# Another order of the SBUF pools in a fused convolution and squared-ReLU MLP kernel

## The chip, the core and the metric

The kernel runs on one NeuronCore of a Trainium2 chip. The core has TensorE (PE, the matmul array, with its weight loads shown as PEld), VectorE (DVE), ScalarE (ACT), GpSimd (POOL) and SyncE (SP), which here only issues DMAs. All of them work on SBUF, an on-chip memory of 128 partitions; a tile has up to 128 rows, one per partition, and in each partition it takes a run of bytes that begins at the same address. PSUM is the small memory into which TensorE writes. The metric is the device time of one execution in microseconds (us), median of three runs.

## What is computed

The input x is 8 sequences of 4096 tokens with 192 features, in float32. First a causal convolution over 7 tokens with softmax weights, one set for each of 8 heads of 24 features; then a two-layer MLP over the 32768 tokens:

```python
w = softmax(weight)                     # (8 heads, 7 taps)
a[t, d] = sum_k w[head(d), k] * x[t - 6 + k, d]
h = a @ w_in                            # 192 -> 2048
g = s * relu(h)**2 + b
out = g @ w_out                         # 2048 -> 192
```

## The kernel before

Features lie on partitions. The 192 features are 128 (tiles with A in their name) and 64 (tiles with B, two blocks of 512 tokens stacked on 128 partitions). The tokens are worked in superblocks of 1024, and each superblock n in two blocks j of 512 tokens. For each block, the 2048 hidden units are worked in 8 pairs p of 128-unit chunks.

The matmuls run in float32r. To reach float32's accuracy, each operand is split into a high and a low part, and the product is made of three: high with low, high with high, low with high. Line numbers are those of the profile:

- `Tokens.load` reads xA and xB from HBM, `conv` (L149, L151) makes the convolution on VectorE into accA and accB, `split_A` and `split_B` write the high and low parts into sA and tB, and `swap` copies them by DMA with the upper and lower 64 partitions exchanged into wA and wB.
- `first` (L526) makes the hidden layer h of one (n, j, p) in PSUM: 18 matmuls of 64 rows x 512 columns, in 9 pairs. One of a pair works on partitions 0 to 63, the other on 64 to 127, at the same time. What streams is sA, wA, tB or wB; what is loaded as weight is a 128-column chunk of the tile W.
- ScalarE takes relu(h) out of PSUM into a tile q (L540) and squares it in place (L547). VectorE rounds it to qh (L549) and takes the rest into ql (L554).
- `second` (L609) multiplies qh and ql with the output weights in W and WB: 20 matmuls of 64 x 512, in 10 pairs, summed in PSUM over the 8 pairs p. It lags behind `first` by LAG = 2 entries of a queue. For superblock 0 `second_whole` (L571 to L578) does the same with 128-row matmuls, and the last entry of all is done by `last` (L668 to L687).
- At the end of a block ScalarE and GpSimd scale and sum the halves (L629 to L642), and SP stores them.
- The weights arrive as float64; the class `Widen` turns them into high and low float32r parts in W and WB during superblock 0. `head` prepares the first tokens, with a part of the convolution on TensorE in plain float32 (L245).

So 2048 bytes in each partition are streamed by every matmul (512 columns of 4 bytes), and 512 bytes (128 columns) are loaded as its weight.

Where the tiles lie is decided by the order of the pools. A pool holds, for each name of a tile, as many buffers as its `bufs` says; pools take their room one after the other, in the order in which they are made, and inside a pool the names follow in the order of their first use, each buffer rounded up to 32 bytes. The pools before, in order: const (W, WB and seven small tiles), raw, wordp, xin, xs, act, qs, outs. In the program built from it, addresses within a partition are:

| tiles | first address | beyond a multiple of 2048 |
|---|---|---|
| W (40960 bytes), WB (8192) | 16512, 57472 | 128 |
| tap, minus, tmax, tsum, sb, bb, bias | 65664 to 66399 | |
| t (2 x 3072), c (3072), words (3 x 6144) | 66400 | 864 or 1888 |
| xA (2 x 4120), xB (2 x 2072) | 94048 | 1888 to 1984 |
| accA, sA, wA, tB, wB, hiB, accB (xs) | 106464 | 2016 |
| q (act), qh and ql (qs), oA, oC, oB, oB2, oA2 (outs) | 155616 | 2016 |

The tiles of xs, act, qs and outs have 2048 or 4096 bytes, so that one offset holds for all their buffers.

Of the kernel before, what the change touches and what calls it, by code (L numbers as in the profile page):

```python
# [9 lines left out]
F32 = mybir.dt.float32  # L10
F32R = mybir.dt.float32r
# [6 lines left out]
P = 128  # L18
# [3 lines left out]
LAG = 2  # L22
# [3 lines left out]
TWICE = (4, 6)  # L26

WARM = (BLK, BLK // 2, BLK // 2)


TOP_MIN = struct.unpack("<f", struct.pack("<I", (1023 - 127) << 20))[0]
# [4 lines left out]
def conv_attention_then_squared_relu_mlp(  # L36
# [25 lines left out]
    NPAIR = weights64.shape[0]  # L62
    K = taps.shape[2]
    PAD = K - 1
    DB = D - P
    NF = 2 * NPAIR
    SUP = 2 * BLK
    NSUP = T // SUP

    const = ctx.enter_context(tc.tile_pool(name="const", bufs=1))  # L70
    raw = ctx.enter_context(tc.tile_pool(name="raw", bufs=2))
    wordp = ctx.enter_context(tc.tile_pool(name="wordp", bufs=3))
    xin = ctx.enter_context(tc.tile_pool(name="xin", bufs=2))
    xs = ctx.enter_context(tc.tile_pool(name="xs", bufs=2))
    act = ctx.enter_context(tc.tile_pool(name="act", bufs=3))
    qs = ctx.enter_context(tc.tile_pool(name="qs", bufs=LAG + 3))
    outs = ctx.enter_context(tc.tile_pool(name="outs", bufs=3))
    ps_h = ctx.enter_context(tc.tile_pool(name="ps_h", bufs=2, space=bass.MemoryType.PSUM))
    ps_o = ctx.enter_context(tc.tile_pool(name="ps_o", bufs=2, space=bass.MemoryType.PSUM))

# [176 lines left out]
    CI = 3 * P  # L257
    CB = CI + 2 * P
    CT = CB + 2 * DB
    W = const.tile([P, NPAIR, 2, CB], F32R, name="W")  # L260
    WB = const.tile([P, NPAIR, 2, 2 * DB], F32R, name="WB")

    def w_in(part, p, chunk, rows):
        return W[rows, p, part, chunk * P : (chunk + 1) * P]

    def w_outA(part, f, rows=slice(0, P)):
        return W[rows, f // 2, part, CI + f % 2 * P :][:, 0:P]

    def w_outB(f, rows=slice(0, P)):
        return WB[rows, f // 2, f % 2, :]  # L270

    class Widen:
# [7 lines left out]
        def parts(self, v):  # L280

            z = min(self.hi, CB)
            yield (*(W[:, self.p, k, self.lo : z] for k in range(2)), v[:, 0 : z - self.lo])
            if self.hi > CB:
                v = v[:, CB - self.lo :].rearrange("p (j d) -> p j d", j=2)
                yield (*(WB[:, self.p, :, k * DB : (k + 1) * DB] for k in range(2)), v)

# [46 lines left out]
    def fetch(p, a=0, z=None):  # L334
        if a == 0:
            words[p] = wordp.tile([P, CT, 2], I32, name="words")
        z = z or CT
        nc.sync.dma_start(
            words[p][:, a:z].rearrange("p f w -> p (f w)"), w_words[p, :, 2 * a : 2 * z]
        )  # L340

    idle = act.tile([P, 2, BLK], F32, name="q")[:, 0, 0:P]
    nc.gpsimd.memset(idle, 0.0)
    tap = const.tile([P, 2, K], F32, name="tap")
    nc.sync.dma_start(tap, taps)
    tapA, tapB = tap[:, 0, :], tap[:, 1, :]
    tok = {0: Tokens(0)}
# [2 lines left out]

    ident = act.tile([P, 2, BLK], F32, name="q")[:, 0, 0:P]
    make_identity(nc, ident)
    minus = const.tile([P, P], F32R, name="minus")
    tmax = const.tile([P, 2], F32, name="tmax")
    tsum = const.tile([P, 2], F32, name="tsum")

    nc.scalar.activation(tsum, idle[:, 0:2], AF.Exp)
    nc.vector.reduce_max(tmax, tap, axis=AX.X)
# [8 lines left out]

    fetch(0, CI, CT)
    fetch(1)
    sb = const.tile([P, 1], F32, name="sb")  # L370
    bb = const.tile([P, 1], F32, name="bb")
    nc.sync.dma_start(sb, s.unsqueeze(0).to_broadcast([P, 1]))
    nc.sync.dma_start(bb, b.unsqueeze(0).to_broadcast([P, 1]))

    def head():
# [4 lines left out]
        warm = ps_o.tile([P, BLK], F32, name="acc1")  # L380
        for cols in WARM:
            nc.tensor.matmul(
# [90 lines left out]
    def column_sums(k):  # L473
# [8 lines left out]
        for o, w in (  # L482
            (sumA, W[:, k, :, CI:CB]),
            (sumB[:, DB:].rearrange("p (j d) -> p j d", j=2), WB[:, k, :, :]),
        ):
            before = W[:, 0, :, CI:CB] if o is sumA else WB[:, 0, :, :]
            before = before.bitcast(F32) if k == 1 else o
# [6 lines left out]
            nc.vector.tensor_tensor(b[:, 0:DB], b[:, 0:DB], b[:, DB:P], op=ALU.add)  # L494


    bias = const.tile([P, 3], F32, name="bias")

    unbiased = []

# [343 lines left out]
```

## Time and profile before

| | |
|---|---|
| median of 3 runs | 2298.05 us (2297.62 to 2298.07) |
| the profiled execution | 2297.88 us, span 2296.1 us |
| TensorE clock granted | 1.000 |
| HBM read, written | 31.64 MB, 25.17 MB |

The span goes from the first to the last instruction that the profiler recorded on the core. A row of the chain of work gives the start and the length of a piece in us, the engine, what it wrote, the line and the number of instructions; a row of the groups gives busy time in us and the mean of one instruction in ns. Three numbers with strokes between them are the shortest, the median and the longest duration of a group in ns. The rows themselves stand in the prediction.

### The profile page before, as it was taken

How to read it: one execution, taken by the hardware profiler on the slowest of the kernel's cores; microseconds unless marked ns; L12 is line 12 of the kernel's file. 1: busy time of each engine (PE TensorE's matmuls, PEld its weight loads, DVE VectorE, ACT ScalarE, POOL GpSimd, SP SyncE). 2: the span in 40 equal slices, each digit the busy share in tenths (PEclk: the TensorE clock that was granted, in tenths of full speed). 3: DMA queues.
4: the chain of work that ended last, by engine and by line, in shares of the span. 5: the costliest groups of instructions: out<-in, count | busy, mean ns of one | idle time of the engine just before them, and what ended most of it. 6: DMA issues, size and time to landing. Idle time of an engine off the chain costs nothing.

```text
span 2296.1 us, 45081 instructions
## 1 busy us (share of the span) xinstructions
PE 2289.9 (100%) x19330; PEld 1829.1 (80%) x19330; DVE 1755.8 (76%) x1995; ACT 1287.5 (56%) x1410; POOL 317.0 (14%) x205
## 2 busy tenths in 40 slices
PE   9999999999999999999999999999999999999999
PEld 6788888888888888888888888888888888888887
DVE  8898777777777787777877777777777777777764
ACT  8755555555555556455555555555555555555554
POOL 0021101101111011110110111101101111011110
PEclk9999999999999999999999999999999999999999
DMA  5113112121121111111111212112121121111110
GB/s 175 38 40 86 42 38 61 49 54 42 43 56 51 51 42 50 49 52 52 44 49 47 55 49 53 47 40 60 49 54 43 43 56 51 51 43 43 42 38 17
DMA packets 46168, 117.51 MB, mean 51 GB/s; under 512 B 7760, under 2 KB 8016, under 8 KB 45968
## 3 DMA queue, kind: packets, MB, share of 16 engines
q1 hardware_dynamic: 45824, 114.50, 18.9%
q8 instruction: 151, 2.47, 0.5%
q14 instruction: 49, 0.40, 0.1%
q10 hardware_dynamic: 144, 0.13, 0.0%
HBM read 31.64 MB, written 25.17 MB: 25 GB/s over the span
## 4 chain that ended last, share of the span: by engine, by line
PE 99%; DVE 1%; DMA 0%; ACT 0%; SPq 0%; issue 0%; DVEq 0%
PE acc L609 50%; PE h L526 47%; PE acc L571 0%; PE acc L572 0%; PE acc L577 0%; PE acc L576 0%; PE acc L578 0%; DVE accA L151 0%; DMA xA<-in_xA 0%; DVE t L303 0%; DVE t L300 0%; DVE t L296 0%; DVE oB L671 0%; ACT W L310 0%; PE acc L668 0%
## 5 line engine op out<-in xcount | busy, mean ns | idle before, releaser
L540 ACT ACTIVATE q<-h 128x1024 f32<-128x1024 f32 x512 | 526.3, 1028 | 966.0 <-PE h L526 958.8
L549 DVE CAST qh<-q 128x1024 fp32r<-128x1024 f32 x497 | 372.8, 750 | 455.6 <-ACT q L547 454.6
L554 DVE TENSOR_TENSOR ql<-q,qh 128x1024 fp32r<-128x1024 f32 x512 | 656.7, 1283 | 56.9 <-ACT qh L549 3.3
L609 PE MATMUL acc<-qh,W 64*128 64x512 f32 x3960 | 622.0, 392 | 0.0
L547 ACT ACTIVATE q<-q 128x1024 f32<-128x1024 f32 x512 | 543.0, 1061 | 16.0
L609 PEld LDWEIGHTS acc<-qh,W 64*128 64x128 f32 x3960 | 370.9, 184 | 91.1
L526 PE MATMUL h<-sA,W 64*128 64x512 f32 x3072 | 441.8, 392 | 0.0
L526 PE MATMUL h<-wA,W 64*128 64x512 f32 x3072 | 441.2, 392 | 0.0
L526 PE MATMUL h<-tB,W 64*128 64x512 f32 x1536 | 439.6, 392 | 0.0
L526 PE MATMUL h<-wB,W 64*128 64x512 f32 x1536 | 439.6, 392 | 0.0
L609 PE MATMUL acc<-ql,WB 64*128 64x512 f32 x1980 | 391.2, 392 | 0.0
L609 PE MATMUL acc<-qh,WB 64*128 64x512 f32 x1980 | 391.1, 392 | 0.0
L609 PE MATMUL acc<-ql,W 64*128 64x512 f32 x1980 | 391.0, 392 | 0.0
L633 POOL TENSOR_TENSOR oB<-oB,oB 128x512 f32<-128x512 f32 x61 | 115.4, 1892 | 1731.7 <-ACT oB L632 1731.7
L151 DVE SCALAR_TENSOR_TENSOR accA<-xA,tap,accA 128x512 f32<-128x512 f32 x378 | 340.5, 901 | 6.8
L526 PEld LDWEIGHTS h<-sA,W 64*128 64x128 f32 x3072 | 287.3, 184 | 72.7 <-issue 1.5
L526 PEld LDWEIGHTS h<-wA,W 64*128 64x128 f32 x3072 | 287.7, 184 | 70.6
L526 PEld LDWEIGHTS h<-tB,W 64*128 64x128 f32 x1536 | 282.6, 184 | 47.1 <-issue 0.2
L526 PEld LDWEIGHTS h<-wB,W 64*128 64x128 f32 x1536 | 282.6, 184 | 23.7
L609 PEld LDWEIGHTS acc<-ql,WB 64*128 64x128 f32 x1980 | 185.5, 184 | 46.0 <-DVE ql L554 0.6
L609 PEld LDWEIGHTS acc<-ql,W 64*128 64x128 f32 x1980 | 185.5, 184 | 45.5
L609 PEld LDWEIGHTS acc<-qh,WB 64*128 64x128 f32 x1980 | 185.5, 184 | 45.4
(115 smaller groups left out, 1035.6 us busy)
## 6 DMA issues: line engine op xcount, KB each, us to landing
wA<-sA SPq DMA_DIRECT2D x126, 256.0 KB, 3.7
outT<-oA SPq DMA_DIRECT2D x63, 256.0 KB, 2.0
wB<-tB SPq DMA_DIRECT2D x60, 256.0 KB, 3.5
xA<-in_xA SPq DMA_DIRECT2D x24, 515.0 KB, 3.6
xB<-in_xB SPq DMA_DIRECT2D x32, 259.0 KB, 2.7
oC<-oB SPq DMA_DIRECT2D x61, 128.0 KB, 2.2
outT<-oC SPq DMA_DIRECT2D x60, 128.0 KB, 2.3
words<-in_w SPq DMA_DIRECT2D x7, 768.0 KB, 6.0
```

The lines of the kernel that those rows point to most:

```text
L151: nc.vector.scalar_tensor_tensor(acc, src, w[:, k : k + 1], acc, op0=ALU.mult, op1=ALU.add)
L526: nc.tensor.matmul(h[:, i, :], w_in(w, p, chunk[0], rows), chunk[part], start=start, stop=stop)
L540: nc.scalar.activation(q, h, AF.Relu)
L547: nc.scalar.activation(q, q, AF.Square)
L549: cast(qh, q)
L554: nc.vector.tensor_tensor(ql, q, qh.bitcast(F32), op=ALU.subtract)
L609: nc.tensor.matmul(accs[to + 2 * i], w(f, r), q[r, f % 2, :], start=start and f == 0, stop=stop and f == ends[i],)
L633: nc.gpsimd.tensor_tensor(o[1], o[1], o[3], op=ALU.add)
```

## The change

The seven small tiles are made first, directly behind the pool const, and an eighth, `gap`, of 296 floats, which nothing writes or reads. Then come the pools qs, xs, act and outs; W and WB move into a pool of their own, wide_w, behind these; raw, wordp and xin, whose buffers have 3072, 6144, 4120 and 2072 bytes, come last. Tiles, buffer counts, instructions and their order stay as they are.

```diff
+GAP = 296
...
     const = ctx.enter_context(tc.tile_pool(name="const", bufs=1))
+    tap = const.tile([P, 2, K], F32, name="tap")
+    minus = const.tile([P, P], F32R, name="minus")
+    tmax = const.tile([P, 2], F32, name="tmax")
+    tsum = const.tile([P, 2], F32, name="tsum")
+    sb = const.tile([P, 1], F32, name="sb")
+    bb = const.tile([P, 1], F32, name="bb")
+    bias = const.tile([P, 3], F32, name="bias")
+    const.tile([P, GAP], F32, name="gap")
+    qs = ctx.enter_context(tc.tile_pool(name="qs", bufs=LAG + 3))
+    xs = ctx.enter_context(tc.tile_pool(name="xs", bufs=2))
+    act = ctx.enter_context(tc.tile_pool(name="act", bufs=3))
+    outs = ctx.enter_context(tc.tile_pool(name="outs", bufs=3))
+    wide_w = ctx.enter_context(tc.tile_pool(name="wide_w", bufs=1))
     raw = ctx.enter_context(tc.tile_pool(name="raw", bufs=2))
     wordp = ctx.enter_context(tc.tile_pool(name="wordp", bufs=3))
     xin = ctx.enter_context(tc.tile_pool(name="xin", bufs=2))
-    xs = ctx.enter_context(tc.tile_pool(name="xs", bufs=2))
-    act = ctx.enter_context(tc.tile_pool(name="act", bufs=3))
-    qs = ctx.enter_context(tc.tile_pool(name="qs", bufs=LAG + 3))
-    outs = ctx.enter_context(tc.tile_pool(name="outs", bufs=3))
...
-    W = const.tile([P, NPAIR, 2, CB], F32R, name="W")
-    WB = const.tile([P, NPAIR, 2, 2 * DB], F32R, name="WB")
+    W = wide_w.tile([P, NPAIR, 2, CB], F32R, name="W")
+    WB = wide_w.tile([P, NPAIR, 2, 2 * DB], F32R, name="WB")
...
-    tap = const.tile([P, 2, K], F32, name="tap")
...
-    minus = const.tile([P, P], F32R, name="minus")
-    tmax = const.tile([P, 2], F32, name="tmax")
-    tsum = const.tile([P, 2], F32, name="tsum")
...
-    sb = const.tile([P, 1], F32, name="sb")
-    bb = const.tile([P, 1], F32, name="bb")
...
-    bias = const.tile([P, 3], F32, name="bias")
```

## The prediction

> **What bounds the kernel now.** I read the page from its first lines, then the chain that ended last, then the waits, and only then single instructions.
>
> ```profile
> span 2296.1 us, 45081 instructions
> PE 2289.9 (100%) x19330; PEld 1829.1 (80%) x19330; DVE 1755.8 (76%) x1995; ACT 1287.5 (56%) x1410; POOL 317.0 (14%) x205
> ...
> PEclk9999999999999999999999999999999999999999
> ...
> PE 99%; DVE 1%; DMA 0%; ACT 0%; SPq 0%; issue 0%; DVEq 0%
> ```
>
> TensorE (PE) is busy all the time and is 99% of the chain, at the full granted clock. A busy PE alone proves little, since its ends are modelled; so the next question is whether it ever waits for anybody, and at what pitch its matmuls follow each other. The list of waits, longest first, answers the first half:
>
> ```profile
> POOL oB L633 <- ACT oB L632: 1731.7, 60, 79.3
> ACT q L540 <- PE h L526: 958.8, 372, 4.7
> DVE qh L549 <- ACT q L547: 454.6, 332, 3.7
> ...
> PEld h L526 <- issue: 1.7, 4, 0.8
> ```
>
> The long waits are those of other engines, ScalarE's for PE's hidden layer among them; PE's own weight loads waited 1.7 us in total in the first matmul stage. So everybody waits for PE, and the time is the number of matmuls times their pitch. The number comes from the groups by line (each pair of 64-row matmuls runs side by side, one on the upper and one on the lower 64 partitions):
>
> ```profile
> L609 PE MATMUL acc<-qh,W 64*128 64x512 f32 x3960 | 622.0, 392 | 0.0
> L526 PE MATMUL h<-sA,W 64*128 64x512 f32 x3072 | 441.8, 392 | 0.0
> L526 PE MATMUL h<-wA,W 64*128 64x512 f32 x3072 | 441.2, 392 | 0.0
> L526 PE MATMUL h<-tB,W 64*128 64x512 f32 x1536 | 439.6, 392 | 0.0
> L526 PE MATMUL h<-wB,W 64*128 64x512 f32 x1536 | 439.6, 392 | 0.0
> L609 PE MATMUL acc<-ql,WB 64*128 64x512 f32 x1980 | 391.2, 392 | 0.0
> L609 PE MATMUL acc<-qh,WB 64*128 64x512 f32 x1980 | 391.1, 392 | 0.0
> L609 PE MATMUL acc<-ql,W 64*128 64x512 f32 x1980 | 391.0, 392 | 0.0
> ...
> L571 PE MATMUL acc<-qh,WB 128*128 128x512 f32 x32 | 13.2, 412 | 0.0
> ```
>
> L526 has 9216 of them, 4608 pairs; L609 has 9900, 4950 pairs; the first block's second stage has five lines of 32 full-height matmuls (L571 stands for them), 160; `last` adds 10 full-height ones. Together 9728 steps. The pitch comes from the chain, whose rows give a start and a length:
>
> ```profile
> 102.42 2.55 PE acc L609 x20
> 104.98 2.10 PE h L526 x18
> ...
> 171.68 4.67 PE acc L609 x40
> 207.15 4.67 PE acc L609 x40
> ...
> 2228.75 4.67 PE acc L609 x40
> ```
>
> Nine pairs of L526 take 2.10 us, 233.3 ns a pair. One block of 512 tokens is 8 x 9 + 8 x 10 = 152 pairs; from 171.68 to 2228.75 there are 58 blocks, so a pair takes 2057.07 / (58 x 152) = 233.34 ns, for all tiles and throughout the run. 9728 x 233.33 ns = 2269.8 us. The first hidden-layer matmul starts at 17.3 us:
>
> ```profile
> L526 PE MATMUL h<-sA,W x3072: 385/391/502, 17.3 to 2282.5; 64*128 64x512 f32 x192
> ...
> 2290.11 0.75 DVE oB L671
> ```
>
> 2269.8 + 17.3 leaves 9.0 us of the span of 2296.1: about 6.0 behind the last matmul (2290.1 to the end) and 3.0 for changes between 64-row and 128-row matmuls and short stalls. The profiled execution took 2297.88 us, 1.8 more than its span, and the median of the three runs is 2298.05; I forecast against 2298.05 and carry the 1.8 along unchanged.
>
> **The change, part by part.** No instruction, wait, queue or buffer count is added, removed or moved: the diff creates the same tiles in other pools and another order, so only addresses inside a partition differ. Nothing is issued by a moved step, and no queue (SP's or POOL's) is passed. In the kernel before, W starts at byte 16512 and the small tiles and the odd-sized pools follow (t 3072 bytes, xA 4120, xB 2072); therefore all tiles from accA on, which hold everything the matmuls stream, start at 2016 beyond a multiple of 2048, and W's chunks at 128 beyond a multiple of 512. After: 64 (tap) + 512 (minus) + 5 x 32 (the five smallest) + 1184 (gap) = 1920, and 16512 + 1920 = 18432 = 9 x 2048. All of qs, xs, act and outs are made of 2048- and 4096-byte buffers, so they and, behind them, W (139264 = 68 x 2048) and WB start at multiples of 2048. Each streamed operand is 2048 bytes long: before, each crosses one 2048-byte boundary 32 bytes after its start; after, none does. t, c, words, xA and xB come last, at other offsets than before.
>
> *VectorE, ScalarE, POOL and DMA: 0.* The convolution is a natural test of VectorE, for its seven taps read the same tile shifted by 4 bytes each:
>
> ```profile
> L151 DVE SCALAR_TENSOR_TENSOR accA<-xA,tap,accA x378: 737/752/1791, 5.6 to 2209.4; 128x512 f32<-128x512 f32 x189
> L151 DVE SCALAR_TENSOR_TENSOR accB<-xB,tap,accB x186: 743/752/754, 81.9 to 2187.2; 128x512 f32<-128x512 f32 x186
> ```
>
> All 186 of accB's lie between 743 and 754 ns, whatever the shift and buffer: 1.5% at most. Where that reaches the path, in the 17.3 us ahead of the first hidden-layer matmul, 1.5% is 0.26 us at most, up or down; I take 0. Elsewhere these engines are covered by PE, and the cover is wide:
>
> ```profile
> 200.00:236.00 36.00, 36.00 (x312) 28.91 (x310) 28.95 (x34) 19.61 (x21) 4.62 (x3) 1.00 0.25 67
> ```
>
> In that stretch VectorE (the third busy time) does 28.95 us of work in 36, and ScalarE 19.61: VectorE would have to become 24% slower before PE waited. The swaps by DMA (wA<-sA, 3.7 us to land on the page) are issued while the convolution runs ahead, a superblock of two 35.5 us blocks before use.
>
> *The weight load: 0.* W's chunks lie 512 bytes apart, so in the kernel before they already start at four different places within 2048 bytes, and one chunk in four (at 1664) crosses a boundary; every pair has the same pitch all the same. And the load is hidden. The one place where loads bind is L507, whose moving operand is a single column:
>
> ```profile
> 160.45 0.19 PEld L609 LDWEIGHTS acc<-qh,WB 64*128 64x128 f32 x2
> 160.56 0.19 PEld L609 LDWEIGHTS acc<-ql,WB 64*128 64x128 f32 x2
> 160.79 0.19 PEld L609 LDWEIGHTS acc<-qh,WB 64*128 64x128 f32 x2
> ```
>
> With nothing streaming, the next load starts 0.11 us after the one before; behind a streamed matmul it waits 0.23. So a load takes some 0.11 us of the 0.233 and is not what sets the pitch.
>
> *The streamed operand: unknown, and the whole case.* The pitch of 233.3 ns is that of streaming 512 columns of float32r. The head's plain float32 matmuls give something to compare:
>
> ```profile
> 5.77 3.60 PE L245 MATMUL acc<-xB,q 128*128 128x512 f32 x8
> ...
> L245 PE MATMUL acc<-xB,q x14: 590/592/697, 4.4 to 10.1; 128*128 128x512 f32 x14
> ```
>
> Eight in 3.60 us, the last 0.592 long: (3.60 - 0.592) / 7 = 429.7 ns for 512 columns. If float32 goes at exactly half the rate of float32r, a pair could take 214.9 ns, and 233.3 holds 18.4 ns (8%) that the slower stream doesn't show. Whether these 18.4 ns hang on the address, no row of before can say, for every float32r operand there has the same offset. Bounds: the change takes away between 0 and 18.4 ns per step, 0 to 9728 x 18.4 = 179.0 us; and below nothing, as no reason excludes a loss. I take 0, by the nearest rows: the convolution's shifts on VectorE, the four places of the weights, and L245 itself, whose taps stream the token tile from seven offsets, each across a 2048-byte boundary, at one duration (590 to 592 ns but for the first). Nowhere in this trace does an address show in a duration.
>
> [...]
>
> Sum: 0 (other engines) + 0 (weights) + 0 (stream) = **2298.0 us**.
>
> **The rivals.**
>
> *The stream does pay for its address: faster.* For it: the 18.4 ns are there in every step without exception, as a fixed start at 2016 would make them, and float32 at half the rate could hide the same bubble. Against it: a constant of the float32r path would look just the same. All removed: 2298 - 179 = 2119 us. Half removed: 2298 - 89 = 2209. Nothing else becomes late at once: at 214.9 ns the 36 us of the stretch above shrink to 33.2, and VectorE has 28.95 in it; but its slack falls from 7 us to 4, so stalls of VectorE would be next. [...]
>
> *Weights and stream now collide: slower.* A load starts beside the matmul it runs under. Before, the load starts at 128 and the stream at 2016, 352 bytes apart modulo 512; after, both start at a multiple of 512. If the two reads hinder each other when they begin at the same offset, each step grows. Bounds: 0 to the whole load of 0.11 us; the nearest row is the 18.4 ns by which the stream is already late, so I price it at as much again: 2298 + 179 = 2477 us. It decides from 0.47 ns per step on (4.6 us in all). Against it: before, the relation of the two offsets modulo 2048 takes four values, and none shows in the pitch.
>
> *The change doesn't do what it says.* The gap tile is never written. If it got no room, the squares would start at 17248, which is 864 beyond a multiple of 2048: the streams would cross a boundary as before, and the time would be 2298 in any of these worlds.
>
> **How the numbers follow.** Same, by the forecast: 0.45; same because the gap gets no room: 0.03; faster: 0.39; slower: 0.13. About 0.2%, 4.6 us, is what a measurement of this kernel can tell from no change. The likeliest case's own range is 2293.5 to 2302.6. The cases of no change hold only 0.48, so the range for 8 in 10 has to take in the faster case with its full bound: 2119 to 2302.6; the slower case, 0.13, is left out. Chances: faster 0.39, same 0.48, slower 0.13.
>
> **What would show it.** The chain's rows of nine pairs of L526: 2.10 us if I am right, 1.93 if the full 18.4 ns go, over 2.10 if loads and stream collide. The distance of two neighbouring blocks' rows of x40: 35.47 us now, 32.7 in the faster case. VectorE's taps should stay at 743 to 754 ns, and the first hidden-layer matmul should start at 17.3 us within 0.3. If the pitch changes at all, the step "streamed operand: 0" is what failed. If PE starts to wait for VectorE, the pitch fell further than VectorE's slack allowed.

## The result and the profile after

The changed kernel takes 2234.55 us (median of 4 runs, 2234.44 to 2234.66) against 2298.01 for the kernel before (now the median of four runs): a ratio of 0.9724, 95% interval 0.9709 to 0.9740. It is 63.5 us faster. Its page, first lines and chain:

```profile
span 2232.9 us, 45081 instructions
...
PE 2226.4 (100%) x19330; PEld 1829.1 (82%) x19330; DVE 1753.5 (79%) x1995; ACT 1286.4 (58%) x1410; POOL 317.8 (14%) x205
...
PE 98%; DVE 1%; ACT 1%; DMA 0%; issue 0%; SPq 0%; DVEq 0%
```

As many instructions on every engine as before, the busy times of VectorE, ScalarE and GpSimd as before within 0.3%, and PE still busy throughout. So it isn't that somebody waits less: PE itself has become faster. The chain of the changed kernel in order of time (start and length in us) says by how much; L526 and L609 are now L531 and L614:

```profile
104.21 2.04 PE h L531 x18
106.25 2.27 PE acc L614 x20
...
169.09 4.53 PE acc L614 x40
203.55 4.53 PE acc L614 x40
...
2201.84 4.53 PE acc L614 x40
```

Nine pairs take 2.04 us where they took 2.10. From 169.09 to 2201.84 are 59 blocks of 152 pairs, 226.67 ns a pair against 233.33. Over 9728 steps that is 64.8 us, and the span fell by 63.2. The other 1.6 us were given back as new short stalls in superblock 0 and just behind it, the largest of them near 100 us, where superblock 0 goes over into superblock 1. The waits of PE and of its weight loads, changed kernel first, then the kernel before (us in total, times, longest):

```profile
PE acc L614 <- DVE ql L559: 0.4, 1, 0.4
...
PEld acc L614 <- DVE ql L559: 1.3, 2, 0.8
```

```profile
PEld acc L609 <- DVE ql L554: 0.6, 2, 0.4
```

A faster PE comes to VectorE's ql too early there: its weight loads wait 1.3 us where they waited 0.6, and PE's own 0.4 ends together with the longest of these waits. From 169.09 us on the 59 blocks follow each other without such a wait, so in the steady part VectorE has room enough. The rest of what the prediction named, the start of the first hidden-layer matmul and VectorE's taps, hasn't moved (shortest, median and longest duration in ns, then first and last start in us):

```profile
L531 PE MATMUL h<-sA,W x3072: 385/386/501, 17.3 to 2219.6; 64*128 64x512 f32 x192
...
L163 DVE SCALAR_TENSOR_TENSOR accB<-xB,tap,accB x186: 742/750/753, 81.2 to 2127.2; 128x512 f32<-128x512 f32 x186
```

### The profile page after: what moved, and what is told of

Same layout as the page of the kernel before. It is cut to its first block, busy times and chain, and to the rows that moved or that the text cites. A ratio compares the mean times of both kernels' runs of the same rounds, so it can differ in the third digit from the quotient of the medians.

```text
span 2232.9 us, 45081 instructions
## 1 busy us (share of the span) xinstructions
PE 2226.4 (100%) x19330; PEld 1829.1 (82%) x19330; DVE 1753.5 (79%) x1995; ACT 1286.4 (58%) x1410; POOL 317.8 (14%) x205
## 4 chain that ended last, share of the span: by engine, by line
PE 98%; DVE 1%; ACT 1%; DMA 0%; issue 0%; SPq 0%; DVEq 0%
PE acc L614 50%; PE h L531 46%; DVE accA L163 0%; PE acc L576 0%; ACT q L552 0%; DVE ql L559 0%; PE acc L577 0%; PE acc L583 0%; PE acc L582 0%; PE acc L581 0%; ACT qh L554 0%; ACT q L545 0%; DMA xA<-in_xA 0%; DVE t L315 0%; ACT oC L589 0%
## 5 line engine op out<-in xcount | busy, mean ns | idle before, releaser
L614 PE MATMUL acc<-qh,W 64*128 64x512 f32 x3960 | 609.9, 386 | 0.0
L614 PEld LDWEIGHTS acc<-qh,W 64*128 64x128 f32 x3960 | 370.9, 184 | 77.9
L531 PE MATMUL h<-sA,W 64*128 64x512 f32 x3072 | 432.4, 387 | 0.0
L531 PE MATMUL h<-wA,W 64*128 64x512 f32 x3072 | 431.6, 386 | 0.0
L531 PE MATMUL h<-tB,W 64*128 64x512 f32 x1536 | 429.9, 386 | 0.0
L531 PE MATMUL h<-wB,W 64*128 64x512 f32 x1536 | 429.9, 386 | 0.0
L614 PE MATMUL acc<-ql,WB 64*128 64x512 f32 x1980 | 385.7, 386 | 0.4 <-DVE ql L559 0.4
L614 PE MATMUL acc<-qh,WB 64*128 64x512 f32 x1980 | 385.6, 386 | 0.0
L614 PE MATMUL acc<-ql,W 64*128 64x512 f32 x1980 | 385.5, 386 | 0.0
L531 PEld LDWEIGHTS h<-sA,W 64*128 64x128 f32 x3072 | 287.3, 184 | 62.9 <-issue 1.1
L531 PEld LDWEIGHTS h<-wA,W 64*128 64x128 f32 x3072 | 287.8, 184 | 60.4
L531 PEld LDWEIGHTS h<-tB,W 64*128 64x128 f32 x1536 | 282.6, 184 | 40.5 <-issue 0.2
L531 PEld LDWEIGHTS h<-wB,W 64*128 64x128 f32 x1536 | 282.5, 184 | 20.1
L614 PEld LDWEIGHTS acc<-ql,WB 64*128 64x128 f32 x1980 | 185.5, 184 | 40.1 <-DVE ql L559 1.3
L614 PEld LDWEIGHTS acc<-ql,W 64*128 64x128 f32 x1980 | 185.5, 184 | 39.0
L614 PEld LDWEIGHTS acc<-qh,WB 64*128 64x128 f32 x1980 | 185.5, 184 | 38.8
```

The lines of the kernel that those rows point to most:

```text
L531: nc.tensor.matmul(h[:, i, :], w_in(w, p, chunk[0], rows), chunk[part], start=start, stop=stop)
L614: nc.tensor.matmul(accs[to + 2 * i], w(f, r), q[r, f % 2, :], start=start and f == 0, stop=stop and f == ends[i],)
```

## The experiments

So an address does count for PE's stream. The change moves everything at once, and three theories were open. A: a stream must start at a multiple of 64 bytes. B: a stream must not cross a 2048-byte boundary. C: it is the weights that must lie at multiples of 512. Four kernels tell them apart. In what follows, a *stage's pitch* is read from the chain: the length of a row of 18 or 20 matmuls, divided by 9 or 10. (Where the two stages lie at different addresses, the steps inside a row are uneven, as the run with distances 256 and 128 will show; the figure of a row is then a mean.)

**Everything 64 bytes further.**

```diff
-GAP = 296
+GAP = 312
```

> The changed kernel with a gap of 312 floats in place of 296: squares, tokens and weights all start 64 bytes beyond a multiple of 2048. Theory A (the streamed operand must start at a multiple of 64 bytes): a pair stays at 226.7 ns, about 2234.6 us. Theory B (the streamed operand must not cross a 2048-byte boundary): each stream crosses one, 233.3 ns, about 2298 us. Theory C (it is the weights' place at multiples of 512 that counts): weights at 64, 233.3 ns, about 2298 us.

Measured: 2234.89 us, ratio to the kernel before 0.9726 (0.9711 to 0.9740). Its chain:

```profile
1000.56 2.04 PE h L531 x18
1002.60 2.27 PE acc L614 x20
```

The pitch is the changed kernel's, though each stream crosses a boundary and the weights are off the multiples of 512. B and C, as stated, fall.

**The old order with 32 bytes more: only the streams move, to multiples of 2048.**

```diff
     bias = const.tile([P, 3], F32, name="bias")
+    const.tile([P, 8], F32, name="pad")
```

> The kernel before with 32 unused bytes behind the small tiles of const: everything streamed moves from 2016 beyond a multiple of 2048 to 0, the weights stay at 128, the order of the pools stays. Theories A and B: 226.7 ns a pair, about 2234.6 us. Theory C: 233.3 ns, about 2298 us.

Measured: 2288.85 us, ratio 0.9960 (0.9946 to 0.9974). The chain:

```profile
1003.51 2.32 PE acc L610 x20
1005.83 2.09 PE h L527 x18
1007.92 2.33 PE acc L610 x20
```

232.4 ns a pair. Every stream starts where it does in the changed kernel, and only a seventh of the gain is there (about 9 us of 63.5). A falls as well.

**The changed kernel with only the weights 32 bytes further.**

```diff
+    wide_w.tile([P, 8], F32, name="pad")
     W = wide_w.tile([P, NPAIR, 2, CB], F32R, name="W")
```

> The changed kernel with 32 unused bytes ahead of W: the weights start 32 beyond a multiple of 512, the streamed tiles stay at multiples of 2048. Theories A and B: 226.7 ns a pair, about 2234.6 us. Theory C: 233.3 ns, about 2298 us. If weights and stream at the same offset hindered each other, it would come out below 2234 us.

Measured: 2297.80 us, ratio 0.9999 (0.9989 to 1.0008): the whole gain is gone, though no streamed tile has moved (only W, WB and the pools behind them, raw, wordp and xin, have). The chain has the pitch of the kernel before:

```profile
1001.09 2.10 PE h L532 x18
1003.19 2.33 PE acc L615 x20
```

**Five offsets at once.** The streamed tiles got pools of their own with unused tiles between them (tB, wB 1024; wA 1536; sA 32; qh 64; ql 96; W 128).

```diff
+    xt = ctx.enter_context(tc.tile_pool(name="xt", bufs=2))
+    shift("to1536", 128)
+    xw = ctx.enter_context(tc.tile_pool(name="xw", bufs=3))
+    shift("to32", 136)
     xs = ctx.enter_context(tc.tile_pool(name="xs", bufs=2))
...
```

> The changed kernel with the streamed tiles at five offsets beyond a multiple of 2048: tB and wB 1024, wA 1536, sA 32, qh 64, ql 96; W at 128. Theory A: sA and ql (offsets that are no multiple of 64) at 392 ns of duration and 233.3 ns of pitch, the others at 386 and 226.7; about 3580 slow steps x 6.67 ns over the changed kernel, 2258 us. Theory B: all cross a boundary, all at 392, about 2298 us. Theory C: weights at 128 as in the kernel before, about 2298 us.

Measured: 2289.74 us in one run, which fits none of the three. The chain:

```profile
1001.86 2.09 PE h L543 x18
1003.95 2.33 PE acc L626 x20
```

No stage reaches 227, not even with tiles at 1024 and 1536. What the fast kernels so far have in common is that weights and streams lie equally far beyond a multiple of 256 or 512 (0 and 0, 64 and 64); before, it was 128 and 480 modulo 512. Hence a fourth theory, D: what counts is the *distance*, the stream's address less the weight's, modulo 512, and only 0 is fast; or E: the same modulo 256. In the mixed kernel the distances modulo 256 are 160 (sA), 128 (wA, tB, wB), 192 (qh) and 224 (ql), none of them 0. The kernels that follow give each stage a distance of its own, by gaps ahead of qs, xs and act, with W at a multiple of 512:

```diff
-GAP = 296
+GAP = 72
...
     qs = ctx.enter_context(tc.tile_pool(name="qs", bufs=LAG + 3))
+    shift("shift1", 128)
     xs = ctx.enter_context(tc.tile_pool(name="xs", bufs=2))
+    shift("shift2", 256)
```

**Distances 256 and 128** (the sizes above).

> The changed kernel with other gaps: the tokens' tiles (streamed in the first stage) start 256 bytes beyond a multiple of 512, the squares (second stage) 128, the weights 0. Theory D (what counts is the distance of stream and weights modulo 512, and only 0 is fast): both stages at 233 ns a pair, about 2298 us. Theory E (the same modulo 256): first stage 226.7, second 233, 2234.6 + 4950 x 6.67 ns = 2268 us. Theory F (each must start at a multiple of 64, and the distance does not count; the kernel before with 32 bytes more already speaks against it): 2234.6 us.

Measured: 2270.36 us. The chain:

```profile
1000.07 2.32 PE acc L621 x20
1002.40 2.06 PE h L538 x18
```

The groups by line (busy us, mean ns of one):

```profile
L621 PE MATMUL acc<-qh,W 64*128 64x512 f32 x3960 | 622.2, 392 | 0.0
...
L538 PE MATMUL h<-sA,W 64*128 64x512 f32 x3072 | 439.1, 390 | 0.0
L538 PE MATMUL h<-wA,W 64*128 64x512 f32 x3072 | 431.9, 386 | 0.0
...
L621 PE MATMUL acc<-qh,WB 64*128 64x512 f32 x1980 | 393.4, 394 | 0.0
L621 PE MATMUL acc<-ql,W 64*128 64x512 f32 x1980 | 391.3, 392 | 0.0
L621 PE MATMUL acc<-ql,WB 64*128 64x512 f32 x1980 | 385.9, 386 | 0.1
```

As means of the rows, the first stage takes 229 ns a pair and the second 232, and the time is near E's 2268. But the steps are uneven. In the kernels where both stages are alike, 386 ns of duration goes with 226.7 of pitch and 392 with 233.3. Here wA has the fast stage's 386, but sA, which the first stage streams first, has 390; and the second stage runs from 386 (ql with WB) to 394 (qh with WB). All weights lie at the same offset, so the distance of a single step doesn't explain this spread. What does is open. It also sets a limit to what follows: beside a slow stage, a row at distance 0 modulo 256 took 2.2 ns a pair more (2.06 us for nine) than in the changed kernel (2.04).

**Distances 32 and 64.**

> As the run with 256 and 128, with the tokens at 32 and the squares at 64 beyond a multiple of 512, the weights at 0. Theory D: both stages at 233 ns a pair, about 2298 us. If the cost grows with the distance from 0, the first stage lies below the second and both between 226.7 and 233 ns. Theory F: first stage 233, second 226.7, 2234.6 + 4608 x 6.67 ns = 2265 us.

Measured: 2277.53 us.

```profile
1003.25 2.30 PE acc L621 x20
1005.55 2.10 PE h L538 x18
```

32 is as slow as before (233), 64 lies between (230). Of the two predictions, neither D's nor F's holds, and the cost doesn't grow with the distance: it is the nearer one that is slow.

**Distances 192 and 320.**

> As the run with 256 and 128, with the tokens at 192 and the squares at 320 beyond a multiple of 512, the weights at 0. Theory D: both stages at 233 ns a pair, about 2298 us. A pitch below 226.7 ns in either stage would show that 0 is not the best distance.

Measured: 2276.54 us.

```profile
1002.98 2.29 PE acc L621 x20
1005.26 2.11 PE h L538 x18
```

192 is slow; 320 gives 229 where 64 gave 230, which fits a period of 256.

**The old order with 160 bytes more: distance 0, weights and streams at 128.**

```diff
     bias = const.tile([P, 3], F32, name="bias")
+    const.tile([P, 40], F32, name="pad")
```

> The kernel before with 160 unused bytes behind the small tiles of const: the streamed tiles and the weights both start 128 bytes beyond a multiple of 512, and the old order of the pools stays. Theory D or E (the distance counts and is 0 here): 226.7 ns a pair, about 2234.6 us. If the order of the pools, or multiples of 64 in both alone, were the cause, it would stay near the 2288.9 us of the kernel before with 32 bytes more.

Measured: 2234.83 us, ratio 0.9726 (0.9709 to 0.9742). One unused tile in the kernel before gives the whole gain, without another order of the pools:

```profile
1000.40 2.04 PE h L527 x18
1002.44 2.27 PE acc L610 x20
```

**Finer distances.** W and WB became larger tiles, used from 16 or 24 bytes on.

```diff
-    W = wide_w.tile([P, NPAIR, 2, CB], F32R, name="W")
+    W = wide_w.tile([P, NPAIR * 2 * CB + 128], F32R, name="W")[:, 4 : 4 + NPAIR * 2 * CB]
+    W = W.rearrange("p (n k c) -> p n k c", n=NPAIR, k=2)
```

> Finer distances: the weights start 16 bytes beyond a multiple of 512, the tokens at 0 (distance 240 modulo 256), the squares at 32 (distance 16). Theory E (distance 0 modulo 256 and nothing else is fast): both stages between 229 and 233 ns a pair, 2256 to 2298 us. Theory H (a granule of 32 bytes or more decides): 16 acts like 0, second stage 226.7. A pitch below 226.7 ns in either stage would show a better distance than 0.

> Finer distances still: the weights start 24 bytes beyond a multiple of 512, the tokens at 32 (distance 8), the squares at 0 (distance 232 modulo 256). Theory E: both stages between 229 and 233 ns a pair, 2256 to 2298 us. Theory H: 8 acts like 0, first stage 226.7 ns. A pitch below 226.7 ns in either stage would show a better distance than 0.

Measured: 2275.64 us and 2287.26 us. The chain of the first and of the second:

```profile
1002.58 2.29 PE acc L623 x20
1004.88 2.10 PE h L540 x18
```

```profile
1002.81 2.32 PE acc L623 x20
1005.12 2.10 PE h L540 x18
```

16 gives 229, 240 gives 233; 8 gives 233, 232 gives 232. A granule of 32 bytes (H) falls, since 8 is slow. No row is below 226.7. But 16 can't be told from 0 here, since a row at distance 0 beside a slow stage took 229 too.

**A shorter load.** Does the weight load that runs beside a stream take the time, in proportion to its length? This kernel leaves out the last 32 of 128 output columns of most matmuls; its result is not the full product, and only its time is of use.

```diff
+                m = slice(0, P if start or stop or n == 0 else 3 * P // 4)
                 nc.tensor.matmul(
-                    h[:, i, :], w_in(w, p, chunk[0], rows), chunk[part], start=start, stop=stop
+                    h[m, i, :], w_in(w, p, chunk[0], rows)[:, m], chunk[part], start=start, stop=stop
...
+                whole = p in (0, NPAIR - 1) or (n, j) == steps[-1][:2]
+                m = slice(0, P if whole else 3 * P // 4)
```

> Leaves out the last 32 of 128 output columns of most matmuls from superblock 1 on (7 of 9 pairs in the first stage, and the second stage at p = 1 to 6), so that these weight loads are 96 columns long and the streams keep their 512. The tokens lie 32 bytes beyond the weights (slow), the squares 0 (fast). [...] If the load's length does not count: 233.3 and 226.7 as before, 2234.6 + 4608 x 6.67 ns = 2265 us.

Measured: 2277.33 us, slower than the 2265 us expected if the length doesn't count. The chain:

```profile
1000.91 2.09 PE h L539 x18
1003.00 2.31 PE acc L624 x20
```

The slow first stage, at distance 32, gained little if anything (232.2 ns a pair; 233.3 with whole loads). The second stage, at distance 0, took 231 where 226.7 was expected. So nothing here speaks for such a proportion: the shorter loads (158 ns each, where whole ones take 184) didn't shorten the pitch. What the shorter load does by itself is not shown. No run has these addresses with whole loads; the row at distance 0 beside a slow stage took 229 with whole loads already; and the matmuls here also write 96 rows in place of 128. That the pitch depends on the weights is shown by the kernel that moved the weights by 32 bytes (2.10 us for nine pairs, where the changed kernel takes 2.04).

**The old order with 416 bytes more: distance 256 in both stages.** With both stages alike no row mixes two pitches, and D and E are told apart cleanly.

```diff
     bias = const.tile([P, 3], F32, name="bias")
+    const.tile([P, 104], F32, name="pad")
```

> The kernel before with 416 unused bytes behind the small tiles of const: the weights start 128 bytes beyond a multiple of 512, everything streamed 384, a distance of 256 in both stages. Theory E (distance 0 modulo 256 is fast): 226.7 ns a pair, about 2234.8 us, as with 160 bytes. Theory D (only 0 modulo 512 is fast): between 228.9 and 233.3 ns, 2256 to 2298 us.

Measured: 2234.57 us, ratio 0.9724 (0.9708 to 0.9740).

```profile
1000.61 2.04 PE h L527 x18
1002.65 2.27 PE acc L610 x20
```

E holds, D falls. All kernels with whole loads but the mixed one, with the pitch from the chain's rows:

| distance modulo 256 | from | ns a pair |
|---|---|---|
| 0 | changed kernel, +64, +160, +416 | 227 |
| 16 | weights at 16, second stage | 229 |
| 64 | 64 and 320, second stages | 230, 229 |
| 128 | old order +32, both stages | 232 |
| 232 | weights at 24, second stage | 232 |
| 8, 32, 96, 224, 240 | weights at 24, first stage; 32, first stage; kernel before; weights at 32; weights at 16, first stage | 233 |
| 192 | 192, first stage | 234 (2.11 / 9) |

Only 0, 96 (kernel before), 128 and 224 (weights at 32) were measured with both stages alike, in several runs each. The others are row means of single runs of kernels whose stages differ, where the row at 0 came out 2.2 ns too high. So the table doesn't tell 16 and 64 from 0, nor 232 from 233; that 8, 32, 192 and 240 are slower than 16 and 64, by 3 to 5 ns, stands out of it.

## Why the prediction was wrong in its step, and where it held

The forecast was no change, 2298.0 us, and it missed: the time fell by 63.5 us. It still lies in the stated range, 2119 to 2302.6, because the range took in the whole of the rival "the stream does pay for its address", to which the prediction gave 0.39. That rival had the sign, but not the cause, so the range held partly by luck.

- *What bounds the kernel* held. The time is 9728 steps times their pitch: with 226.67 in place of 233.33 the same sum gives the measured fall within 1.6 us. Two slips in the reading change nothing: 2057.07 / 8816 is 233.33, not 233.34, and the 1.7 us of the first stage's weight loads is one row of three, which come to 2.8 (1.7 + 0.7 + 0.4).
- *Other engines, DMA: 0* held, with VectorE's taps at 742 to 753 ns (743 to 754 before) and the first hidden-layer matmul at 17.3 us. VectorE's times show nothing of these addresses, and so they were no test of PE.
- *The streamed operand: 0* is the step that failed. It was argued from "Nowhere in this trace does an address show in a duration". The bound beside it was the right one: 0 to 18.4 ns, of which 6.67 went; it is an estimate that takes float32 at half the rate of float32r, which no run shows. The rival that the stream pays for its address had the sign and 36% of its full price (64.8 of 179.0 us). But its mechanism was wrong too: a stream at multiples of 2048 alone gave 9 us (old order with 32 bytes more).
- *The weight load: 0* failed as an argument, though the load is indeed hidden (0.11 us of 0.23). W's chunks lie 512 bytes apart, and the four places that I counted are all the same place modulo 256. The trace of before held one single distance, 96, in every step, so its uniform pitch could say nothing about distances. Moving the weights by 32 bytes costs the whole gain (2297.80 us, where the changed kernel takes 2234.55). The convolution on TensorE (L245) has seven distances, but in float32, at 429.7 ns a step; it told nothing of a stream nearly twice as fast (226.7 to 233.3 ns).
- *Weights and stream collide* named the right pair and the wrong sign. I priced the same offset as the bad case; it is the best one measured (226.7 ns a pair).
- *The gap gets no room* has nothing for it: unused tiles of the same kind do move what lies behind them (32 bytes gave 2288.85 us, 160 gave 2234.83). And its 2298 doesn't follow. With or without the gap, W lies 139264 - 18432 = 59 x 2048 bytes behind the squares, so the distance would be 0 either way, and by the rule found here the changed kernel would be as fast without the gap. No run left it out.

Shown is: the pitch hangs on the distance of stream and weight. With both stages alike it is 226.7 ns at distance 0 modulo 256, in four kernels, and 232.4 to 233.3 at 96, 128 and 224; the absolute offset (weights at 0, 64 or 128) and the crossing of a 2048-byte boundary don't count where the distance is 0 (2234.55 to 2234.89 us). By what means the distance acts is not shown. Why the period is 256, why 16 and 64 are better than 8 and 32, why the steps are uneven where the stages differ, and what the 11.8 ns are that stay at distance 0 above half of float32's 429.7, is open.

## What to carry to other kernels

Where PE is the bound and streams float32r with a weight load beside every matmul, look at the addresses that the allocator gave, and try streamed operand and weights that start equally far beyond a multiple of 256 bytes (226.7 ns a pair here, 232.4 to 233.3 at distances 96, 128 and 224); that other kernels gain by it is not shown here. In this kernel one unused tile of 160 bytes was worth 2.7%, as much as the new order of all pools. And before a uniform duration is read as "addresses don't matter", count how many different values of the suspected quantity the trace really holds: here it was one.

## What the runs showed of the hardware that was not expected

A load that is hidden in time (0.11 us from load to load with nothing streaming, 0.23 behind a stream) still bears on the pitch of the stream over it: by the place of its weights alone it was 226.7 or 233.3 ns for 512 float32r columns. The pitch doesn't follow the distance smoothly (0: 227, 8: 233, 16: 229, 32: 233, 64: 230, 128: 232, some of them row means). And loads of 96 columns in place of 128 didn't shorten it: 232 and 231 ns in the two stages.
